# Gate products over 512 rows, spectrum sums on GpSimd, and early loads in another order

## The chip, the cores and the metric

One core of one Trainium2 chip. The metric is device time in microseconds (us) of one execution, the median of nine. "The profile" is one execution taken by the hardware profiler. Its clock starts at the first instruction of the program.

## The reference, cut to what matters

```
xn = layernorm(x)                               # x: 2048 rows x 640, bf16
A  = irfft2(rfft2(xn) * (w_r + 1j * w_i))       # over rows and columns; w: 2048 x 321
B  = ((xn @ w_gate) * (xn @ w_up)) @ w_down     # 640 -> 1536 -> 640
out = x + A + B
```

A (the filter branch) and B (the gated branch) both read xn and are independent until the last sum.

## The kernel before, in words

Each step is a *task*: a name, an engine or two, a cost in nanoseconds from a table, a priority, and the buffers that it reads and writes. A planner (class `_Sched`) runs on the host while the program is built. It lays the tasks on PE, ACT, DVE, GpSimd (POOL) and the SP queue by those costs, hands out the eight PSUM banks, and writes the waits. On the chip each engine then runs its list **in the planner's order**: an instruction whose input is late holds back all that stands behind it on that engine. Numbers behind a name are a block of 128 rows, a group, or a spectrum tile.

- **Loads.** SP issues `ld_x0` to `ld_x5` (blocks 0, 1, 2, 3, 4 to 7, 8 to 15) mixed with the weight loads `ld_gw…`, then tables (`ld_sm`, one load on ACT's queue, holds the identity and two small matrices; `ld_fd`, `ld_tf`, `ld_g`, `ld_ti`), filter rows `ld_w0…` to `ld_w3…`, and only then the transposes `xt4` to `xt15`. Later filter rows `ld_w4…` on wait for a ring of four slots.
- **Layernorm.** Blocks 0 to 7: `bn`, `ag` on DVE (L769 to L775). Blocks 8 to 15: `sm`, `sq` on ACT (L756, L762). Then `ve`, `sd`, `rs`, `sub`, `mul` (L788 to L810).
- **Transposed xn.** Blocks 0 to 3 by PE (`T0`, L828; copied out by `eT0`, L709/L710), blocks 4 to 15 by DMA (`xt`, L816).
- **Gated branch.** `GU` (L951): for one of twelve tiles of 128 gate features and a chunk of rows, five matmuls give gate and five give up, side by side in **one** PSUM bank. Chunks are 128, 128 and then seven times 256 rows. ACT copies the bank out (`eG`, L709), and for each pair of feature tiles DVE multiplies gate by up (`H`, L966). `GU` has a low priority and fills PE where the other branch waits. Last comes `ACC` (L1172): twelve matmuls of 320 columns for each block and half.
- **Filter branch, forward.** `S1` to `S5` on DVE (L865 to L899) and `R` on PE (L912; reads the second matrix of `sm`) for eight pairs of blocks.
- **Filter branch, middle, for tiles t = 0 to 15.** `D` on PE (L994), `eD` on ACT, `C` on PE (L1015 to L1018), `WM` on DVE (L1030, L1033: times the filter, reads PSUM), `CB` on DVE (L1045 to L1049: sums and differences of the four products), `NG` on ACT (L1054 to L1056: negated copies), `IA` on PE (L1070, L1071), `eIA` on ACT. The products lie in a ring of two, the results of `CB` and `NG` in a ring of two.
- **Filter branch, back.** `I` on PE (L1099), `eI` on ACT into a ring of two (`TC`), `V1` to `V5` on DVE for each pair of blocks, `IV` on PE (L1180: adds A into the bank of `ACC`), `FIN` on DVE (L1187: adds x), stores.

The early part of the step that the change moves to GpSimd is:

```
c.e.tensor_tensor(v_y[:, r2, 512:768], p01[:, 0:256], p10[:, 0:256], _OP.add)               # L1045
c.e.scalar_tensor_tensor(v_y[:, r2, 896:961], p01[:, 256:321], -1.0, ...)                   # L1046
c.e.tensor_tensor(v_y[:, r2, 768:833], p00[:, 256:321], p11[:, 256:321], _OP.subtract)      # L1048
return c.e.tensor_tensor(v_y[:, r2, 256:512], p00[:, 0:256], p11[:, 0:256], _OP.subtract)   # L1049
```

Of the kernel before, what the change touches and what calls it, by code (L numbers as in the profile page):

```python
# [15 lines left out]
_DMA_LAT = 1000.0  # L16
_DMA_ISSUE = 440.0
# [488 lines left out]
_CHUNKS = ((0, 1), (1, 1), (2, 2), (4, 2), (6, 2), (8, 2), (10, 2), (12, 2), (14, 2))  # L506
_LP = 321
_SN = math.sin(2.0 * math.pi / 5.0)
# [8 lines left out]
def _d_dve(n):  # L517
    return n * 1.04 + 65.0


def _d_dve_psum(n):
    return n * 1.04 + 70.0
# [14 lines left out]
def _d_act(n):  # L537
    return n * 0.833 + 80.0
# [8 lines left out]
def _build(nc, A_x, A_w_r, A_w_i, B_w_gate, B_w_up, B_w_down, out, opts=None):  # L547
# [3 lines left out]
    with es:  # L551
# [8 lines left out]
        sch.caps = {"glu": opts.get("cap_glu", 2), "acc": opts.get("cap_acc", 4), "fill": 1}  # L560
        lay = {}
# [43 lines left out]
        b_p = alloc("P", 2 * 4 * 2 * _LP)  # L605
        b_y = alloc("Y", 2 * 1024)
        o_end = max(o_end, cur[0])
        cur[0] = o_3
        b_tc = alloc("TC", 2 * 2560)
        b_vt = alloc("VT", 2 * 2048)  # L610
# [44 lines left out]
        v_p = V("P").bitcast(_F32).rearrange("p (r w c l) -> p r w c l", r=2, w=2, c=2)  # L655
        v_y = V("Y").rearrange("p (r n) -> p r n", r=2)
        v_tc = V("TC").bitcast(_F32).rearrange("p (r s u n) -> p r s u n", r=2, s=5, u=2)
# [54 lines left out]
        dma("ld_sm", V("SM"), d_sm.rearrange("p t n -> p (t n)"), 128 * 768, [(b_sm, None)], prio=0.002, q="act")  # L712
# [34 lines left out]
        for gi, (b0, nb) in enumerate(_X_LOADS):  # L747
            dma("ld_x%d" % gi, v_x[:, b0:b0 + nb, :], xv[:, b0:b0 + nb, :], 128 * nb * 1280,
                [(b_x, ("s", b0, b0 + nb))], prio=(0.0, 0.01, 0.02, 0.03, 0.042, 0.06)[gi])
        muls = {}  # L750
        for gi, (b0, nb) in enumerate(_LN_GROUPS):
            pbase = 1.0 + 0.05 * gi if gi < 4 else opts.get("ln_prio", 5.99) + 0.05 * (gi - opts.get("ln_lead", 3))
            for b in range(b0, b0 + nb):
# [13 lines left out]
                else:  # L767
                    def em_bn(c, b=b):
                        c.e.bn_stats(v_st[:, b, 0:6], v_x[:, b, 0:320])  # L769
                        return c.e.bn_stats(v_st[:, b, 6:12], v_x[:, b, 320:640])  # L770
                    T("bn%d" % b, "dve", 800.0, em_bn, reads=[(b_x, ("s", b, b + 1))],
                      writes=[(b_st, ("b", b, b + 1))], prio=pbase)
# [3 lines left out]
                    T("ag%d" % b, "dve", 130.0, em_ag, reads=[(b_st, ("b", b, b + 1))],  # L776
                      writes=[(b_mv, ("b", b, b + 1))], prio=pbase)
            if b0 >= opts.get("act_stats", 8):
                def em_mb(c, sl_=slice(b0, b0 + nb)):
                    c.e.tensor_copy(v_mv[:, sl_, 0], v_m32[:, sl_])  # L780
                    return c.e.tensor_scalar(v_mv[:, sl_, 1], v_ss[:, sl_], 1.0 / _D, None, _OP.mult)
                T("mb%d" % b0, "dve", 160.0, em_mb, reads=[(b_m32, ("b", b0, b0 + nb)), (b_ss, ("b", b0, b0 + nb))],
                  writes=[(b_mv, ("b", b0, b0 + nb))], prio=pbase)
# [5 lines left out]
            T("ve_%d" % gi, "dve", 80.0, em_ve, reads=[(b_mv, gk)], writes=[(b_ve, gk)], prio=pbase - 0.006)  # L789
# [3 lines left out]
            T("sd_%d" % gi, "act", 120.0, em_sd, reads=[(b_ve, gk)], writes=[(b_sd, gk)], prio=pbase - 0.006)  # L793
# [3 lines left out]
            T("rs_%d" % gi, "dve", 80.0, em_rs, reads=[(b_sd, gk)], writes=[(b_rs, gk)], prio=pbase)  # L797

            for b in range(b0, b0 + nb):
# [4 lines left out]
                T("sub%d" % b, "dve", 290.0, em_sub, reads=[(b_mv, ("b", b, b + 1))],  # L804
# [6 lines left out]
                muls[b] = T("mul%d" % b, ("dve", "act") if b >= 4 else "dve", {"dve": 290.0, "act": _d_act(640) + 93}, em_mul, reads=[(b_rs, ("b", b, b + 1))],  # L811
                  writes=[(b_x, ("s", b, b + 1))], prio=pb)

                if b >= opts.get("xt_dma", 4):
                    def em_xt(c, b=b):
                        return c.e.dma_start_transpose(v_xt[:, :, b * 128:(b + 1) * 128], v_x[:, b, :])  # L816
                    T("xt%d" % b, "sp", opts.get("xt_issue", 1500.0), em_xt, reads=[(b_x, ("s", b, b + 1))],
                      writes=[(b_xta, ("s", b * 128, (b + 1) * 128)), (b_xtb, ("s", b * 128, (b + 1) * 128))], prio=pb, nbytes=128 * 1280)
                    continue
# [11 lines left out]
                t0 = T("T0_%d" % b, "pe", 5 * _d_mm(128), em_t0, reads=[(b_x, ("s", b, b + 1)), (b_sm, None)],  # L831
                       prio=pb, bank="pair" if b < opts.get("e0_split", 2) else "single", cls="a")

                if b < opts.get("e0_split", 2):
# [9 lines left out]
                    hold(t0, es_)  # L844
                    continue
# [10 lines left out]
        for g in range(8):  # L856
# [46 lines left out]
            for u in range(2):  # L903
                def em_r(c, gr=gr, u=u):
                    bk = bank_of(c.t)
                    ins = None
                    for k, (f, o) in enumerate(((0, 1), (1, 0), (1, 1), (0, 0), (2, 0))):
# [8 lines left out]
                       reads=[(b_f, ("r", 3 * gr, 3 * gr + 3)), (b_sm, None)], prio=pf, bank="pair", cls="a")  # L916
# [18 lines left out]
        units = sorted((max(c_at[ci], w_at[ft + 1]), ci, ft) for ci in range(len(_CHUNKS)) for ft in range(0, 12, 2))  # L935
        for ui, (at_, ci, ft0) in enumerate(units):
# [6 lines left out]
            for u in range(2):  # L943
                ft = ft0 + u

# [8 lines left out]
                gu = T("GU_%d_%d" % (ft, b0), "pe", 10 * _d_mm(n), em_gu,  # L954
# [10 lines left out]
            def em_h(c, ft0=ft0, rr=rr, n=n, rows=rows):  # L965
                return c.e.tensor_tensor(v_ht[:, ft0:ft0 + 2, rows], v_gbf[:, rr, :, 0:n], v_gbf[:, rr, :, n:2 * n],  # L966
                                         _OP.mult)
            T("H_%d" % ui, "dve", _d_dve_tt16(2 * n), em_h,
# [4 lines left out]
        for q in range(2):  # L973
            dma("ld_ti%d" % q, v_ti[:, 8 * q:8 * q + 8], d_ti[:, 8 * q:8 * q + 8], 128 * 8 * 512,
                [(b_wd, ("e", 2048 * q, 2048 * q + 2048))], prio=9.0 + 0.3 * q)

        for t in range(16):
            pq = 10.0 + 0.05 * t
            ar = t % 3
            r2 = t % 2  # L980
            wr = t % _NW
            for w_ in range(2):
                for h in range(2):
# [3 lines left out]
                        semkey=("w", wr), after=[wpad])  # L987
# [34 lines left out]
            def em_wm(c, tc=tc, r2=r2, wr=wr):  # L1022
                bk = bank_of(tc)
                ins = None
                for h in range(2):
# [3 lines left out]
                    for w in range(2):  # L1029
                        c.e.tensor_tensor(  # L1030
                            v_p[:, r2, w, :, 128 * h:128 * h + 128].rearrange("p c (m k) -> p c m k", k=4),
                            xh.rearrange("p c (m k) -> p c m k", k=4), wv[:, w].unsqueeze(1).to_broadcast([128, 2, 32, 4]), _OP.mult)
                ins = c.e.tensor_tensor(  # L1033
                    v_p[:, r2, :, :, 256:321], ps[:, bk:bk + 2, 256:321].unsqueeze(1).to_broadcast([128, 2, 2, 65]),
# [4 lines left out]
                   writes=[(b_p, ("r", r2, r2 + 1))], prio=pq - 0.001, frees=tc)  # L1039
            hold(tc, wm)  # L1040

            def em_cb(c, r2=r2):
                p00, p01, p10, p11 = (v_p[:, r2, 0, 0], v_p[:, r2, 0, 1], v_p[:, r2, 1, 0], v_p[:, r2, 1, 1])

                c.e.tensor_tensor(v_y[:, r2, 512:768], p01[:, 0:256], p10[:, 0:256], _OP.add)  # L1045
                c.e.scalar_tensor_tensor(v_y[:, r2, 896:961], p01[:, 256:321], -1.0, p10[:, 256:321], _OP.mult,  # L1046
                                         _OP.subtract)
                c.e.tensor_tensor(v_y[:, r2, 768:833], p00[:, 256:321], p11[:, 256:321], _OP.subtract)  # L1048
                return c.e.tensor_tensor(v_y[:, r2, 256:512], p00[:, 0:256], p11[:, 0:256], _OP.subtract)  # L1049
            T("CB_%d" % t, "dve", 2 * _d_dve(256) + 2 * _d_dve(65), em_cb,  # L1050
              reads=[(b_p, ("r", r2, r2 + 1))], writes=[(b_y, ("r", 2 * r2, 2 * r2 + 1))], prio=pq - 0.001)

            def em_ng(c, r2=r2):
                c.e.activation(v_y[:, r2, 0:256], v_y[:, r2, 512:768], _ACTF.Copy, scale=-1.0)  # L1054
                c.e.activation(v_y[:, r2, 833:896], v_y[:, r2, 897:960], _ACTF.Copy, scale=-1.0)
                return c.e.activation(v_y[:, r2, 961:1024], v_y[:, r2, 769:832], _ACTF.Copy)  # L1056
            T("NG_%d" % t, "act", _d_act(256) + 2 * _d_act(63), em_ng,
              reads=[(b_y, ("r", 2 * r2, 2 * r2 + 1))], writes=[(b_y, ("r", 2 * r2 + 1, 2 * r2 + 2))],
              prio=pq - 0.001)

            def em_ia(c, t=t, r2=r2):
                bk = bank_of(c.t)
                ins = None
                for k in range(5):
                    if k < 4:
                        l1, l2 = v_y[:, r2, 256 + k:768:4], v_y[:, r2, k:512:4]
                    else:
                        l1, l2 = v_y[:, r2, 768:896], v_y[:, r2, 896:1024]
# [4 lines left out]
            ia = T("IA_%d" % t, "pe", 10 * _d_mm(128), em_ia, reads=[(b_y, ("r", 2 * r2, 2 * r2 + 2)), (b_wd, ("e", 256 * t, 256 * t + 256))],  # L1073
# [11 lines left out]
        for f0, f1 in _WD_LOADS:  # L1085
            dma("ld_wd%d" % f0, v_wd[:, f0:f1], wdv[:, f0:f1], 128 * (f1 - f0) * 1280,
                [(b_wd, ("e", 640 * f0, 640 * f1))], prio=18.0 if f0 < 7 else 9.6)
        for a in range(16):
# [15 lines left out]
            gr = (a // 2) % 2  # L1104
            un = a % 2

            def em_ei(c, ti=ti, gr=gr, un=un):
                bk = bank_of(ti)
                return copy_on(c, v_tc[:, gr, :, un, :],
                               psflat[:, bk * 512: bk * 512 + 640].rearrange("p (s n) -> p s n", s=5))  # L1110
            ei = T("eI_%d" % a, ("act", "dve"), {"dve": _d_dve_psum(640), "act": _d_act(640)}, em_ei,
                   writes=[(b_tc, ("r", 2 * gr + un, 2 * gr + un + 1))], prio=pa - 0.001, frees=ti)
# [5 lines left out]
            def em_v1(c, gr=gr):  # L1118
                b1r, b1i, b2r, b2i = [v_tc[:, gr, i].rearrange("p u n -> p (u n)") for i in range(4)]
# [5 lines left out]
            T("V1_%d" % b_, "dve", 4 * _d_dve(256), em_v1, reads=[(b_tc, ("r", 2 * gr, 2 * gr + 2))],  # L1125
              writes=[(b_vt, ("r", gr, gr + 1))], prio=pa - 0.001)

            def em_v2(c, gr=gr):
                a_ = v_tc[:, gr, 4].rearrange("p u (o b) -> p (u o) b", o=2)
# [3 lines left out]
              reads=[(b_vt, ("r", gr, gr + 1)), (b_tc, ("r", 2 * gr, 2 * gr + 2))],  # L1133
# [25 lines left out]
        for a in range(16):  # L1159
# [4 lines left out]
            for hf in range(2):  # L1164
# [14 lines left out]
                def em_iv(c, ag2=ag2, a=a, sl3=sl3):  # L1179
# [3 lines left out]
                       reads=[(b_v, ("a", a, a + 1)), (b_sm, None)], prio=pc + 0.01 + 0.001 * hf - 22.0, after=[ag2])  # L1183
# [13 lines left out]
        sch.affinity = opts.get("affinity", 600.0)  # L1197
# [79 lines left out]
```

## Time and profile before

| | |
|---|---|
| median of nine runs | 213.32 us (212.78 to 214.1) |
| the profiled execution | 214.05 us; span of its instructions 212.3 us |
| busy, share of the span | PE 96%, DVE 87%, ACT 57%, POOL 0% |
| granted PE clock | 1.000 |
| stage 0 to 15.18 us | first loads, layernorm of blocks 0 to 3, first `GU` |
| stage 15.18 to 88.79 us | rest of layernorm, `S`/`R`, `GU` up to the first `D` |
| stage 88.79 to 143.50 us | the sixteen tiles of the middle, `GU` between them |
| stage 143.50 to 209.67 us | `I`, the last `GU`, `V`, `ACC` |
| stage 209.67 to 212.30 us | last `FIN` and stores |

How to read it: PE's matmuls are pipelined, so a matmul's listed duration overlaps the next one's. What a run of matmuls takes is read from one start to the next, as the chain that ended last does. Idle time of an engine costs only where PE, or the end, waits for it.

### The profile page before, as it was taken

How to read it: one execution, taken by the hardware profiler on the slowest of the kernel's cores; microseconds unless marked ns; L12 is line 12 of the kernel's file. 1: busy time of each engine (PE TensorE's matmuls, PEld its weight loads, DVE VectorE, ACT ScalarE, POOL GpSimd, SP SyncE). 2: the span in 40 equal slices, each digit the busy share in tenths (PEclk: the TensorE clock that was granted, in tenths of full speed). 3: DMA queues.
4: the chain of work that ended last, by engine and by line, in shares of the span. 5: the costliest groups of instructions: out<-in, count | busy, mean ns of one | idle time of the engine just before them, and what ended most of it. 6: DMA issues, size and time to landing. Idle time of an engine off the chain costs nothing.

```text
span 212.3 us, 5204 instructions
## 1 busy us (share of the span) xinstructions
PE 202.9 (96%) x2044; PEld 169.6 (80%) x2044; DVE 185.2 (87%) x536; ACT 122.0 (57%) x281; POOL 0.2 (0%) x4
## 2 busy tenths in 40 slices
PE   8799999699999999989999999999999899999994
PEld 8789899588898998978888888898766677667773
DVE  3699989799999989389999999947999999999821
ACT  2375899699866756778999897786222202200000
POOL 0000000000000000000000000000000000000000
PEclk9999999999999999999999999999999999999999
DMA  6999999531133000002224223025033223222411
GB/s 188 302 341 396 385 302 204 110 62 31 34 61 59 8 3 0 0 11 57 60 54 119 60 62 90 3 62 154 3 106 97 64 61 110 80 76 64 127 47 46
DMA packets 30456, 21.74 MB, mean 102 GB/s; under 512 B 10336, under 2 KB 29408, under 8 KB 30304
## 3 DMA queue, kind: packets, MB, share of 16 engines
q1 hardware_dynamic: 28320, 20.34, 35.5%
q10 hardware_dynamic: 2112, 1.08, 2.0%
q8 instruction: 16, 0.26, 0.5%
q14 instruction: 8, 0.07, 0.1%
HBM read 16.82 MB, written 2.62 MB: 92 GB/s over the span
## 4 chain that ended last, share of the span: by engine, by line
PE 63%; DVE 22%; DMA 7%; issue 3%; ACT 1%; SPq 1%; DVEq 0%
PE ps L951 38%; PE ps L1172 12%; DMA arena<-in_A_x_dram 4%; DMA arena<-arena 3%; PE ps L1070 2%; PE ps L1071 2%; DVE arena L1187 2%; PE ps L994 2%; PE ps L912 2%; DVE arena L1144 1%; DVE arena L1145 1%; SPq L703 1%; DVE arena L1153 1%; DVE arena L966 1%; DVE arena L1137 1%
## 5 line engine op out<-in xcount | busy, mean ns | idle before, releaser
L709 ACT ACTIVATE arena<-ps 128x512 bf16<-128x512 f32 (+5 forms) x189 | 99.9, 572 | 55.9 <-PE ps L1099 28.2
L951 PE MATMUL ps<-arena 128*128 128x256 bf16 (+1 forms) x1080 | 112.8, 261 | 3.2 <-DMA arena<-arena 1.9
L951 PEld LDWEIGHTS ps<-arena 128*128 128x128 bf16 x1080 | 93.6, 98 | 14.5 <-DMA arena<-arena 2.1
L1172 PE MATMUL ps<-arena 128*128 128x320 bf16 x384 | 56.5, 299 | 0.3 <-DVE arena L1187 0.3
L1172 PEld LDWEIGHTS ps<-arena 128*128 128x128 bf16 x384 | 37.2, 98 | 14.7 <-DVE arena L1187 0.7
L966 DVE TENSOR_TENSOR arena<-arena 128x512 bf16<-128x512 bf16 (+1 forms) x54 | 21.1, 391 | 11.1 <-ACT arena L709 11.0
L1030 DVE TENSOR_TENSOR arena<-ps,arena 128x256 f32<-128x256 f32 x64 | 22.6, 418 | 0.0
L1187 DVE TENSOR_TENSOR arena<-ps,arena 128x320 bf16<-128x320 f32 x32 | 15.6, 486 | 6.7 <-PE ps L1180 6.7
L1070 PE MATMUL ps<-arena 128*128 128x128 bf16 x80 | 10.6, 219 | 0.0
L1071 PE MATMUL ps<-arena 128*128 128x128 bf16 x80 | 10.6, 219 | 0.0
L1180 PE MATMUL ps<-arena 128*128 128x320 bf16 x32 | 9.1, 300 | 0.6 <-DVE arena L1154 0.4
L1070 PEld LDWEIGHTS ps<-arena 128*128 128x128 bf16 x80 | 8.7, 112 | 0.5
L865 DVE TENSOR_TENSOR arena<-arena 128x384 f32<-128x384 bf16 x16 | 8.8, 553 | 0.0
L1071 PEld LDWEIGHTS ps<-arena 128*128 128x128 bf16 x80 | 8.7, 112 | 0.0
L769 DVE BATCH_NORM_STATS2 arena<-arena 128x6 f32<-128x320 bf16 x8 | 3.9, 491 | 3.7 <-DMA arena<-in_A_x_dram 3.7
L1033 DVE TENSOR_TENSOR arena<-ps,arena 128x260 f32<-128x260 f32 x16 | 7.1, 445 | 0.0
L1045 DVE TENSOR_TENSOR arena<-arena 128x256 bf16<-128x256 f32 x16 | 6.8, 423 | 0.2
L1054 ACT ACTIVATE arena<-arena 128x256 bf16<-128x256 bf16 x16 | 6.6, 414 | 0.3 <-DVE arena L1049 0.2
L1049 DVE TENSOR_TENSOR arena<-arena 128x256 bf16<-128x256 f32 x16 | 6.7, 421 | 0.0
L866 DVE TENSOR_TENSOR arena<-arena 128x256 f32<-128x256 bf16 x16 | 6.7, 420 | 0.0
L1152 DVE TENSOR_TENSOR arena<-arena 128x640 bf16<-128x640 f32 x8 | 6.6, 821 | 0.1
L762 ACT ACTIVATE arena<-arena 128x640 bf16<-128x640 bf16 x8 | 6.6, 827 | 0.0
(71 smaller groups left out, 213.1 us busy)
## 6 DMA issues: line engine op xcount, KB each, us to landing
arena<-in_A_x_dram SPq DMA_DIRECT2D x20, 160.0 KB, 2.4
out_dram<-arena SPq DMA_DIRECT2D x32, 80.0 KB, 1.6
arena<-c_tf SPq DMA_DIRECT2D x4, 384.0 KB, 11.3
arena<-in_A_w_r_dram SPq DMA_DIRECT2D x32, 40.1 KB, 2.3
arena<-in_A_w_i_dram SPq DMA_DIRECT2D x32, 40.1 KB, 2.2
arena<-in_B_w_gate_dram SPq DMA_DIRECT2D x4, 320.0 KB, 7.8
arena<-in_A_x_dram SPq DMA_DIRECT2D x1, 1280.0 KB, 12.2
arena<-c_ti SPq DMA_DIRECT2D x2, 512.0 KB, 14.0
```

The source lines that it names most:

```text
L709: return c.e.activation(dst, src, _ACTF.Copy)
L865: c.e.tensor_tensor(uo[:, o, :, 0:3, :], v_xb[:, b:b + 2, 0:6:2, :], v_xb[:, b:b + 2, 5:10:2, :], op)
L951: ins = c.e.matmul(ps[:, bk, w * n:(w + 1) * n], v_gw[:, w, j, ft, :], v_xt[:, j, rows], start=(j == 0), stop=(j == 4))
L966: return c.e.tensor_tensor(v_ht[:, ft0:ft0 + 2, rows], v_gbf[:, rr, :, 0:n], v_gbf[:, rr, :, n:2 * n], _OP.mult)
L1030: c.e.tensor_tensor(v_p[:, r2, w, :, 128 * h:128 * h + 128].rearrange("p c (m k) -> p c m k", k=4), xh.rearrange("p c (m k) -> p c m k", k ...
L1033: ins = c.e.tensor_tensor(v_p[:, r2, :, :, 256:321], ps[:, bk:bk + 2, 256:321].unsqueeze(1).to_broadcast([128, 2, 2, 65]), v_w[:, wr, :, 0 ...
L1045: c.e.tensor_tensor(v_y[:, r2, 512:768], p01[:, 0:256], p10[:, 0:256], _OP.add)
L1070: c.e.matmul(dst, l1, v_ti[:, t, 0, :], start=True, stop=False)
L1071: ins = c.e.matmul(dst, l2, v_ti[:, t, 1, :], start=False, stop=True)
L1172: ins = c.e.matmul(ps[:, bk, 0:320], v_ht[:, ft, a * 128:(a + 1) * 128], v_wd[:, ft, sl3], start=(ft == 7), stop=False)
L1180: return c.e.matmul(ps[:, bank_of(ag2), 0:320], v_sm[:, 2, :], v_v[:, a, sl3], start=False, stop=True)
L1187: return c.e.tensor_tensor(v_out[:, a % 2, sl3], ps[:, bk, 0:320], v_xr[:, xs, sl3], _OP.add)
```

## The change

Four parts; in each, the planner's cost table and limits change with it, so that the whole order is planned anew.

1. **Chunks.** Rows 512 to 2047 are taken in three chunks of 512. For these, one `GU` is five matmuls of 512 columns that fill a whole bank with gate *or* up (named `GU_f_row_0` and `_1`); `H` covers one feature tile and 512 rows. A chunk needs four transposed blocks before its first matmul.
2. **Sums on GpSimd.** `CB` keeps the two operations of 256 columns (L1045, L1049) and goes to POOL. The two of 65 columns become `CD` on DVE. `NG` waits for both. The rings of products and of results become three deep, and so does `TC`.
3. **Early loads.** `ld_x1` goes ahead of the first weights. `ld_sm` is split: the identity stays on ACT's queue, the rest (`ld_sm1`) goes on SP behind `ld_x5`. `ld_ti`, all `ld_w` and `ld_wd` wait for the last layernorm `mul15`, so the transposes stand ahead of them on SP. `bn` is two tasks, and the second of block 1 waits for the copy of the first transposed block.
4. **Planner.** Entries of its cost table are changed (most of those of DVE, ACT and DMA are raised); at most two tasks of class "a" hold banks at once; ACT is preferred over DVE for copies by 1500 ns, not 600.

In the order that results, PE runs `T0_1` behind `GU_3_0`, `R_0` behind `GU_3_2`, and `I_6`, `I_7` ahead of `ACC_0_0`. ACT runs `sm8` between the two copies of `GU_2_2` and `GU_3_2`. POOL runs `CB_0` to `CB_15`.

```diff
-_CHUNKS = ((0, 1), (1, 1), (2, 2), (4, 2), (6, 2), (8, 2), (10, 2), (12, 2), (14, 2))
+_CHUNKS = ((0,1),(1,1),(2,2),(4,4),(8,4),(12,4))
...
+        sch.caps["a"] = opts.get("cap_a", 2)
...
-        b_p = alloc("P", 2 * 4 * 2 * _LP)
-        b_y = alloc("Y", 2 * 1024)
+        b_p = alloc("P", 3 * 4 * 2 * _LP)
+        b_y = alloc("Y", 2 * _YS)
+        b_y3 = alloc("Y3", _YS, at=lay["STAT"][0])
...
+        b_tc3 = alloc("TC3", 2560, at=lay["GBF"][0])
...
-        dma("ld_sm", V("SM"), d_sm.rearrange("p t n -> p (t n)"), 128 * 768, [(b_sm, None)], prio=0.002, q="act")
+        dma("ld_sm0", v_sm[:, 0, :], d_sm[:, 0, :], 128 * 256, [(b_sm, ("t", 0, 1))], prio=0.002, q="act")
+        dma("ld_sm1", v_sm[:, 1:3, :], d_sm[:, 1:3, :], 128 * 512, [(b_sm, ("t", 1, 3))], prio=0.25)
...
+                if nb == 4:
+                    def em_gu4(c, ft=ft0, w=u, rows=rows):
+                        bk = bank_of(c.t)
+                        for j in range(5):
+                            ins = c.e.matmul(ps[:, bk, :], v_gw[:, w, j, ft, :], v_xt[:, j, rows], start=(j == 0),
+                                             stop=(j == 4))
+                        return ins
...
+                c.e.tensor_tensor(v_y[ar][:, 512:768], p01[:, 0:256], p10[:, 0:256], _OP.add)
+                return c.e.tensor_tensor(v_y[ar][:, 256:512], p00[:, 0:256], p11[:, 0:256], _OP.subtract)
+            ce = opts.get("cb_eng", "pool")
+            T("CB_%d" % t, ce, {"dve": 2 * _d_dve(256), "pool": opts.get("cb_pool", 1600.0)}, em_cb,
...
-                        semkey=("w", wr), after=[wpad])
+                        semkey=("w", wr), after=[wpad, muls[opts.get("w_after", 15)]])
...
-        sch.affinity = opts.get("affinity", 600.0)
+        sch.affinity = opts.get("affinity", 1500.0)
```

## The prediction

> **What bounds the kernel now.** I read the page first: PE is busy throughout, DVE nearly so.
>
> ```profile
> PE 202.9 (96%) x2044; PEld 169.6 (80%) x2044; DVE 185.2 (87%) x536; ACT 122.0 (57%) x281; POOL 0.2 (0%) x4
> PE   8799999699999999989999999999999899999994
> DVE  3699989799999989389999999947999999999821
> ```
>
> Busy is no proof of being the limit, so I took the lengths of PE's runs from the chain that ended last (start, length, what).
>
> ```profile
> 22.15 0.56 PE ps L912 x10
> 98.84 1.09 PE ps L951 x10
> 191.90 1.63 PE ps L1172 x12
> ```
>
> Ten matmuls of 128 columns take 0.56 us, ten of 256 take 1.09, twelve of 320 take 1.63: 0.056, 0.109 and 0.136 each, that is 0.417 ns a column and 2.5 ns a matmul. In the same view `C` (four of 321) takes 0.55 and `IV` 0.137. Now the work from 15.18 us, where the last `T0` has ended, stage by stage, against the windows.
>
> ```profile
> 15.18:88.79 73.61, 71.53 (x753) 63.35 (x751) 67.40 (x201) 57.32 (x123) 0.00 (x0) 1.00 0.48 123
> 88.79:143.50 54.71, 54.13 (x596) 47.74 (x594) 49.20 (x161) 46.49 (x123) 0.00 (x0) 1.00 0.23 56
> 143.50:209.67 66.17, 64.32 (x518) 46.50 (x516) 58.35 (x139) 11.37 (x18) 0.00 (x0) 1.00 0.27 82
> ```
>
> First stage: 14 `GU` of 128 rows (7.8), 53 of 256 (57.9), 16 `R` (4.5): 70.2 of 73.6 us. Middle: 16 x (`D` 0.28 + `C` 0.55 + `IA` 0.56) = 22.2 and 29 `GU` (31.7): 53.9 of 54.7. Last: 16 `I` (4.5), two `GU` (2.2), 32 `ACC` with `IV` (56.7): 63.4 of 66.2. So PE has work for 187.5 of 194.5 us, and **all that can be won behind the start is 7.0 us of stalls (3.4, 0.8, 2.8) and the fixed part of the matmuls**. Where the stalls lie, PE's and SP's timelines say:
>
> ```profile
> 9.54 4.43 PE L951 MATMUL ps<-arena 128*128 128x128 bf16 x70 [0.18 <-DMA arena<-in_B_w_gate_dram]
> 21.98 0.72 PE L912 MATMUL ps<-arena 128*128 128x128 bf16 x10
> 39.75 6.91 PE L951 MATMUL ps<-arena 128*128 128x256 bf16 x60 [1.85 <-DMA arena<-arena]
> 158.82 0.45 PE L1180 MATMUL ps<-arena 128*128 128x320 bf16 x2 [0.42 <-DVE arena L1154]
> 161.32 0.72 PE L1099 MATMUL ps<-arena 128*128 128x128 bf16 x10 [0.29 <-DVE arena L1131]
> 29.21 1.18 SPq L703 DMA_DIRECT2D arena<-in_A_w_r_dram  x2
> 32.25 21.58 SPq L816 DMA_TRANSPOSE arena<-arena  x8
> ```
>
> PE stands 2 us at 38 to 39.75 for the first transpose, which SP issued at 32.25 behind the filter loads; later it waits for `V5` and `V2` on DVE.
>
> **Chunks of 512.** A matmul of 512 columns is 0.417 x 512 + 2.5 = 216 ns, so a `GU` of five takes 1.08 where ten of 256 took 1.092: 72 of them save 0.9 us. Bank copies and `H` stay at 512 columns. But the first one needs blocks 4 to 7, not 4 and 5. DVE's queue says when the last, `mul7`, comes: from `S1_0` (14.7, as before) the list up to it is `S_0` 5.5, `S1` to `S3` of group 1 4.2, eight `bn` at 0.40, eight `H` at 0.21 and three at 0.33, `ag`, four `sub` and `mul` at 0.30, small ones: 19 us, so 34 to 35.5 with some waits for ACT. With 2.6 us to land (the median of the page) `xt7` is there at 37 to 38, and PE arrives at 37.5 to 39 (below). The 2.0 us stall goes; its cover is thin.
>
> **Early loads.** Two answers in opposite directions. `GU_0_0` starts about 0.9 earlier (7.8 to 6.9), because the copy it waits for no longer stands behind `bn` of block 1. But `T0_1` now stands behind `GU_2_0`, whose weights land at 9.5 (the row at 9.54): PE idles from 8.0 to 9.4, then 0.5 more for the copies of `T0_1`. Summed row by row, the last `T0` ends at 15.4 instead of 15.18: **+0.2**. Then `R_0` needs `ld_sm1`, queued behind the 1280 KB of x:
>
> ```profile
> arena<-in_A_x_dram SPq DMA_DIRECT2D x1, 1280.0 KB, 12.2
> arena<-c_fd SPq DMA_DIRECT2D x1, 160.5 KB, 11.1
> ```
>
> Issued at 12.06 and 13.54, these landed at 24.3 and 24.6; `ld_sm1` comes between them. PE reaches `R_0` at 15.4 + 6 x 0.56 + 4 x 1.09 = 23.1: **+1.2**, a stall that was not there (`R` started at 21.98). `sm8` waits for the same x on ACT from 22.6 on, with a bank copy behind it, and PE's next `GU` wait for that: +0.6 more. Moving the filter loads behind the transposes costs nothing: 19 loads at 0.6 us on SP after the last transpose (67 us) are issued by 80, and `C_0` comes at about 88; if the transposes slipped 6 us it would begin to cost. `R_2` to `R_6` meet DVE within half a microsecond either way: +0.6, from 0 to 2.
>
> First stage after: 7.8 + 12 x 1.092 + 41 x 1.08 + 4.5 = 69.7, stalls 2.4 (3.4 before).
>
> **Sums on GpSimd.** DVE loses two rows of 0.34 us each tile:
>
> ```profile
> L1045 DVE TENSOR_TENSOR arena<-arena 128x256 bf16<-128x256 f32 x16 | 6.8, 423 | 0.2
> L1049 DVE TENSOR_TENSOR arena<-arena 128x256 bf16<-128x256 f32 x16 | 6.7, 421 | 0.0
> L1054 ACT ACTIVATE arena<-arena 128x256 bf16<-128x256 bf16 x16 | 6.6, 414 | 0.3 <-DVE arena L1049 0.2
> ```
>
> 16 x 0.67 = 10.7 us leave DVE, at a place where PE is the limit (0.8 us of stalls), so this buys no time there by itself. What POOL takes no row shows; its only rows set one column. Bounds: 0.67 for both if it kept DVE's pace; 1.66 if it read one operand at a time at ACT's 0.41 for 256. I take 1.6, near the upper row, and carry 3.3 as the rival's. The path that counts is from `C_t` to `IA_t`: `WM` 1.75, `CB` 1.6, `NG` 0.6, handovers 0.4, queueing on DVE and ACT 0.8: 5.2 us. In PE's order at the densest place (t = 7 to 11) there stand between them `D` 3, `GU` 3, `IA` 2, `C` 2 = 6.3 us, so 1.1 us of cover; a lower `CB` gains nothing. But the pace there is one tile in 2.47 us (1.39 + one `GU`), where ACT's timeline gives `eD` 0.71 + `eIA` 0.62 + `NG` 0.60 + a bank copy 0.55 = 2.48 and SP's 4 x 0.62 for filter rows: no room. Middle stage after: 22.2 + 27 x 1.08 = 51.4, stalls 1.5 (0.5 to 4).
>
> The Trainium skill, GPSIMD Engine Reference, section 3.1, gives about 2.6 cycles an element for a two-input operation; an estimate from it is 1.2 us for the pair, and the sum stays as it is. Against this change speaks SBUF — State Buffer, section "Who interferes with whom": a VectorE operation with two SBUF inputs and a GpSimd operation that reads SBUF shut each other out for a whole instruction. `CD` and `H` are such; one GpSimd operation of 0.6 us waited for in each tile would put 9.6 us back on DVE, 49 us of the stage's 51.4, and still not make it the end. No row here shows it.
>
> **Rings of three.** Last stage: `I_6`, `I_7` go early and `I` waits for a `V2` two pairs back. DVE needs 5.5 for `V` and 1.2 to 1.6 for `FIN` a pair, PE 7.6. Laying both lists out from `I_0` I find waits of 0.1 and 0.2 at `IV`, 0.5 and 0.4 at `I`: 1.2 us instead of 2.8. Work: 4.5 + 4 x 1.08 + 56.7 = 65.5.
>
> **Sum.** 15.4 + 69.7 + 51.4 + 65.5 = 202.0, stalls 2.4 + 1.5 + 1.2 = 5.1, tail 2.6 as before: a span of 209.7 against 212.3. The profiled execution took 214.05, 1.75 more than its span, so 211.45; it lies 0.7 above the median, so the median should be **210.7**.
>
> **Rivals.** (1) *The stalls all but go* (1.5 us in all: `ld_sm1` lands early, DVE keeps ahead of `R`): 207.1. For it: every stage has spare DVE time on average; against it: the landing of x. (2) *Slower by GpSimd*: at 3.3 us a `CB`, 16 x 3.3 = 53 us is the middle stage's 52.9, and the path becomes 6.9, 0.6 over its cover. From there POOL is the bound: at 3.6 the stage is 57.6 plus about 1 to fill, 5.7 over forecast, 216.4. For it: no row of POOL exists and DVE's two-input rows run at the same time; against: 3.3 is five times DVE's rows. (3) *One wait for another*: `mul7` late by 2 us, `R` late on DVE, the start at +0.2: the first stage keeps 4.5 us of stalls, 2.1 more than forecast: 212.8. (4) *The change doesn't do what it says* can't be where POOL's list holds all `CB`.
>
> **How the numbers follow.** 0.3% (0.64 us) is about what a measurement of this kernel can tell from no change. Chances: forecast 0.52, rival 1 0.16, rival 2 and its like 0.23, rival 3 0.09. Faster 0.68, same 0.09, slower 0.23. The range for 8 in 10 goes from rival 1, 207.1, into rival 2, 215.5.
>
> **What would show it.** Right: `R_0` (L912 by its new number) starting at 24.3 to 24.7 with PE idle before it; no idle over 0.5 before the first matmul of 512 columns, at 37.5 to 39.5; ten matmuls of 512 in 2.16 us; the first `I` at 139 to 141.5; POOL start to start 0.6 to 0.9 within a pair. Wrong: POOL busy over 50 us with PE waiting for ACT's `NG`; `xt7` landing after 40.

## The result and the profile after

The change made the kernel slightly **slower**: 213.96 us (213.66 to 214.51, fifteen runs) against 213.0 for the kernel before (47 runs, the nine above among them); ratio 1.0044, 95% interval 1.0034 to 1.0055. Forecast: 210.7, faster.

The page of the profile after, the lines that answer to those of before:

```profile
PE 202.2 (95%) x1684; PEld 135.2 (64%) x1684; DVE 185.5 (87%) x504; ACT 122.1 (58%) x281; POOL 22.5 (11%) x36
PE   8889999999999999999997889999999999999994
DVE  4699899999999997399899997966999999999921
```

Two 256-column sums a tile have left DVE, and DVE is busy for 185.5 us, where it was 185.2. And PE has a hole in the middle that it did not have. The windows, by the same three stages (from the end of the last `T0`, here 15.58, to `D_0`, to `I_0`, to PE's end; length, then PE, PEld, DVE, ACT, POOL busy):

```profile
15.58:86.27 70.69, 70.36 (x548) 43.58 (x546) 66.73 (x200) 56.80 (x122) 0.00 (x0) 1.00 0.47 126
86.27:143.10 56.83, 53.02 (x440) 32.40 (x439) 50.01 (x128) 45.92 (x121) 22.32 (x32) 1.00 0.22 54
143.10:209.27 66.17, 65.78 (x517) 46.83 (x516) 57.92 (x138) 12.73 (x21) 0.00 (x0) 1.00 0.27 82
```

Stalls, as the sum of the time by which each start-to-start step of PE's matmuls exceeds the matmul's own length (0.417 ns a column + 2.5 ns), to about 0.1: 3.5, 1.0 and 2.9 us before, 1.2, **5.6** and 0.9 after. The first and last stage won about 4.3 us, the middle gave 4.6 back. What PE waited for there, by its timeline (the last field is the idle time and its releaser; L1066 is `WM`'s last row):

```profile
117.36 1.25 PE L962 MATMUL ps<-arena 128*128 128x512 bf16 x5 [1.57 <-DVE arena L1066]
123.17 0.73 PE L1027 MATMUL ps<-arena 128*128 128x128 bf16 x10 [0.93 <-DVE arena L1066]
```

These two are 2.5 of the 5.6 us; the view of PE's waits names 0.6 more for `WM` and 0.7 for `NG` on ACT. So PE waits mostly for DVE's `WM`, in the stage from which DVE's work was taken. The groups of the middle stage say why; first `CD`'s two rows before (L1046, L1048), in a second fence after (L1086, L1088), with `H` (L998), `WM` (L1063) and the sums on POOL:

```profile
L1048 DVE TENSOR_TENSOR arena<-arena 128x65 bf16<-128x65 f32 x16 | 3.6, 224 | 0.0
L1046 DVE SCALAR_TENSOR_TENSOR arena<-arena 128x65 bf16<-128x65 f32 x16 | 3.6, 223 | 0.0
```

```profile
L1063 DVE TENSOR_TENSOR arena<-ps,arena 128x256 f32<-128x256 f32 x64 | 22.5, 411 | 0.0
L1079 POOL TENSOR_TENSOR arena<-arena 128x256 bf16<-128x256 f32 x16 | 11.6, 725 | 0.0
L1078 POOL TENSOR_TENSOR arena<-arena 128x256 bf16<-128x256 f32 x16 | 11.3, 707 | 117.7 <-DVE arena L1066 117.7
L1088 DVE TENSOR_TENSOR arena<-arena 128x65 bf16<-128x65 f32 x16 | 11.3, 705 | 0.0
L998 DVE TENSOR_TENSOR arena<-arena 128x512 bf16<-128x512 bf16 x14 | 7.5, 535 | 7.9 <-ACT arena L714 7.9
L1086 DVE SCALAR_TENSOR_TENSOR arena<-arena 128x65 bf16<-128x65 f32 x16 | 6.3, 393 | 0.3
```

The same 65 columns took 224 ns and take 705, as long as the row of 256 columns on POOL beside them. DVE's and POOL's timelines of one tile show it:

```profile
93.80 0.66 DVE L1086 SCALAR_TENSOR_TENSOR arena<-arena 128x65 bf16<-128x65 f32 x1
94.38 0.77 DVE L1088 TENSOR_TENSOR arena<-arena 128x65 bf16<-128x65 f32 x1
95.07 1.07 DVE L1063 TENSOR_TENSOR arena<-ps,arena 128x256 f32<-128x256 f32 x3
```

```profile
93.62 0.75 POOL L1078 TENSOR_TENSOR arena<-arena 128x256 bf16<-128x256 f32 x1 [1.16 <-DVE arena L1066]
94.34 0.73 POOL L1079 TENSOR_TENSOR arena<-arena 128x256 bf16<-128x256 f32 x1
```

In this tile each row of `CD` ends 0.09 us behind the POOL row that was running, and the next row of `WM` starts 0.01 us behind POOL's second. So it goes in six tiles; in the ten others `CD`'s first row starts 0.05 us ahead of POOL and takes its 0.23, and only the second is held up. From `CD`'s first start to its last end it is 0.81 us in the ten tiles and 1.35 in the six, 1.01 on average. All of `CB` (the two long sums included) took 1.03 before. **GpSimd relieved DVE of 16 x 0.02 us.** And three rows of `H` that met POOL took 0.96 us each where `H` took 0.42 before, 1.6 us in all: DVE has more busy time in the stage than before, 50.0 us where it was 49.2. `WM`, which reads one operand from PSUM, is untouched: the 21 of its rows (L1063) that overlap a POOL row last 406 to 413 ns, the others 407 to 425. This agrees with the rule of the Trainium skill, SBUF — State Buffer, section "Who interferes with whom", which the prediction weighed.

### The profile page after: what moved, and what is told of

Same layout as the page of the kernel before. It is cut to its first block, busy times and chain, and to the rows that moved or that the text cites. A ratio compares the mean times of both kernels' runs of the same rounds, so it can differ in the third digit from the quotient of the medians.

```text
span 212.0 us, 4504 instructions
## 1 busy us (share of the span) xinstructions
PE 202.2 (95%) x1684; PEld 135.2 (64%) x1684; DVE 185.5 (87%) x504; ACT 122.1 (58%) x281; POOL 22.5 (11%) x36
## 4 chain that ended last, share of the span: by engine, by line
PE 61%; DVE 21%; SPq 6%; DMA 5%; ACT 3%; POOL 1%; issue 1%; ACTq 0%; DVEq 0%
PE ps L962 26%; PE ps L1213 22%; DVE arena L1063 9%; PE ps L982 6%; SPq L708 6%; DMA arena<-c_sm 5%; DVE arena L1088 3%; ACT arena L714 3%; DVE arena L1066 2%; PE ps L924 2%; PE ps L1138 2%; PE ps L1221 2%; DVE arena L1086 2%; DVE arena L998 2%; POOL arena L1079 1%
## 5 line engine op out<-in xcount | busy, mean ns | idle before, releaser
L962 PE MATMUL ps<-arena 128*128 128x512 bf16 x360 | 83.1, 379 | 1.6 <-DVE arena L1066 1.6
L962 PEld LDWEIGHTS ps<-arena 128*128 128x128 bf16 x360 | 33.6, 98 | 37.9 <-DVE arena L1066 1.9
L1213 PEld LDWEIGHTS ps<-arena 128*128 128x128 bf16 x384 | 37.3, 98 | 14.4
L982 PE MATMUL ps<-arena 128*128 128x128 bf16 (+1 forms) x360 | 28.2, 237 | 1.5 <-DMA arena<-in_B_w_gate_dram 1.0
L982 PEld LDWEIGHTS ps<-arena 128*128 128x128 bf16 x360 | 24.9, 98 | 4.0 <-DMA arena<-in_B_w_gate_dram 1.3
L998 DVE TENSOR_TENSOR arena<-arena 128x512 bf16<-128x512 bf16 x36 | 16.7, 464 | 10.6 <-ACT arena L714 10.6
L1078 POOL TENSOR_TENSOR arena<-arena 128x256 bf16<-128x256 f32 x16 | 11.3, 707 | 117.7 <-DVE arena L1066 117.7
L1063 DVE TENSOR_TENSOR arena<-ps,arena 128x256 f32<-128x256 f32 x64 | 22.5, 411 | 0.0
L1109 PE MATMUL ps<-arena 128*128 128x128 bf16 x80 | 10.7, 220 | 1.3 <-ACT arena L1095 0.7
L1109 PEld LDWEIGHTS ps<-arena 128*128 128x128 bf16 x80 | 8.6, 111 | 5.2 <-ACT arena L1095 2.3
L1079 POOL TENSOR_TENSOR arena<-arena 128x256 bf16<-128x256 f32 x16 | 11.6, 725 | 0.0
L1088 DVE TENSOR_TENSOR arena<-arena 128x65 bf16<-128x65 f32 x16 | 11.3, 705 | 0.0
L1110 PE MATMUL ps<-arena 128*128 128x128 bf16 x80 | 10.7, 219 | 0.0
L777 DVE BATCH_NORM_STATS2 arena<-arena 128x6 f32<-128x320 bf16 x16 | 7.2, 478 | 3.4 <-DMA arena<-in_A_x_dram 3.1
L1110 PEld LDWEIGHTS ps<-arena 128*128 128x128 bf16 x80 | 8.8, 112 | 0.7
L1027 PE MATMUL ps<-arena 128*128 128x128 bf16 (+1 forms) x80 | 6.8, 219 | 0.9 <-DVE arena L1066 0.9
```

The lines of the kernel that those rows point to most:

```text
L962: ins = c.e.matmul(ps[:, bk, :], v_gw[:, w, j, ft, :], v_xt[:, j, rows], start=(j == 0), stop=(j == 4))
L982: ins = c.e.matmul(ps[:, bk, w * n:(w + 1) * n], v_gw[:, w, j, ft, :], v_xt[:, j, rows], start=(j == 0), stop=(j == 4))
L998: return c.e.tensor_tensor(v_ht[:, ft0, rows], v_gbf[:, rr, 0, :], v_gbf[:, rr, 1, :], _OP.mult)
L1063: c.e.tensor_tensor(v_p[:, ar, w, :, 128 * h:128 * h + 128].rearrange("p c (m k) -> p c m k", k=4), xh.rearrange("p c (m k) -> p c m k", k ...
L1079: return c.e.tensor_tensor(v_y[ar][:, 256:512], p00[:, 0:256], p11[:, 0:256], _OP.subtract)
L1088: return c.e.tensor_tensor(v_y[ar][:, 768:833], p00[:, 256:321], p11[:, 256:321], _OP.subtract)
```

## Experiments

Theory A: GpSimd's reads hold up `CD` (and some `H`); DVE gets no time back, and PE, in an order laid out for a relieved DVE, waits for `WM`. Rival B: the way from `C` to `IA` over GpSimd is too long. Rival C: the order is bad by itself. "Same order" means that every engine's list is kept as planned, and the edit is made behind `sch.plan`.

**1. CD first.** One wait more:

```diff
+            cb, cd = by["CB_%d" % i], by["CD_%d" % i]
+            cb.deps.add(cd)
...
```

> The changed kernel, every engine's order kept, but CB on GpSimd waits until CD of its tile has ended on DVE. Theory A: CD no longer meets its tile's CB, its two rows fall from 393 and 705 ns to about 225 each, DVE gets 0.65 us a tile back, some H may still be held up, and the middle stage's stalls fall from 5.6 to between 1 and 2.5 us: 209.3 to 211 us. Rival B: CB starts about 0.45 us later, so the way from C to IA is longer still: 214.5 or more. Rival C: 213.5 to 214.5.

Measured: **208.88 us**, ratio to the kernel before 0.9805 (0.9783 to 0.9828), 5.1 us less than the changed kernel. Its groups, and its windows for the middle stage:

```profile
L1086 DVE SCALAR_TENSOR_TENSOR arena<-arena 128x65 bf16<-128x65 f32 x16 | 3.6, 227 | 0.3
L1088 DVE TENSOR_TENSOR arena<-arena 128x65 bf16<-128x65 f32 x16 | 3.6, 222 | 0.0
```

```profile
87.31:138.97 51.66, 51.66 (x440) 32.96 (x439) 38.76 (x128) 45.30 (x121) 21.65 (x32) 1.00 0.27 59
```

`CD` is back at 0.36 us from start to end, DVE at 38.8 us where it was 50.0, PE without a hole. The gain is larger than A's range (209.3 to 211) allowed: 0.5 us of stalls are left in the stage, not 1 to 2.5. B and C fall: `CB` started later, in the same order, and the time fell. This version beats both kernels.

**2. The sums back on DVE**, same order:

```diff
+            sch.order["pool"].remove(cb)
+            dve.insert(dve.index(wm) + 1, cb)
...
```

> The changed kernel with its order on PE, ACT and SP kept as it is, and only CB put back on DVE, directly behind WM. Theory A (given back): GpSimd's reads hold up CD on DVE, so DVE never got the freed time, and PE's order, laid out for a DVE with 0.67 us less a tile, runs into WM. CB and CD then cost DVE 0.67 + 0.28 = 0.95 us a tile where the held-up CD costs 0.39 + 0.71 = 1.10, so most of the middle stage's 5.6 us of stalls stay: 212.3 to 213.7 us. Rival B (long path): the pair on GpSimd makes the way from C to IA too long; that way gets about 0.5 to 0.8 us shorter, and the stalls go: 209.3 to 211. Rival C (the order itself is bad, wherever the sums run): 213.5 to 214.5.

Measured: 213.25 us (ratio 1.0005, 0.9993 to 1.0017), middle stalls 4.9 us. As A says: a DVE that does the sums itself is as late as one that is held up by them.

**3. The sums on DVE, planned anew**, that is the other parts of the change without GpSimd:

```diff
-            ce = opts.get("cb_eng", "pool")
+            ce = opts.get("cb_eng", "dve")
```

> The changed kernel with CB on DVE, and the planner laying out the order with DVE's true load: the change without its GpSimd part. A, B and C agree here that the middle stage falls back to about the 1.0 us of stalls of the kernel before, while the 2.4 us won in the first stage, the 2.0 in the last and the 0.9 of fixed matmul parts stay: 209.2 to 210.5 us. At 212.5 or more the other parts would be worth nothing, and the prediction would be wrong in more than one step.

Measured: 213.91 us (1.0040, 1.0024 to 1.0055). All three theories missed. PE had no gate products left at the end of the stage and stood idle, and the granted clock (the last but two of the numbers) was lower behind that; the windows at that place:

```profile
140.00:145.00 5.00, 2.41 (x26) 1.53 (x23) 2.57 (x9) 3.44 (x9) 0.00 (x0) 1.00 0.24 66
145.00:149.50 4.50, 4.46 (x36) 3.62 (x37) 2.59 (x8) 3.09 (x5) 0.00 (x0) 0.62 0.61 182
```

The lower clock is not what cost most of it: in two of the nine runs it was 1.000 over the whole execution, not 0.992, and they took 213.47 and 213.88 us, the other seven 213.76 to 214.65.

**4. The same with four gate products kept for that place**, ahead of `sch.plan`:

```diff
+        for u in range(2):
+            by["GU_10_12_%d" % u].deps.add(by["C_15"])
+            by["GU_11_12_%d" % u].deps.add(by["IA_%d" % (14 + u)])
...
```

> The run with the sums on DVE and a new plan (213.91 us) showed PE idle for 1.74 and 0.89 us at the end of the middle stage, behind its last gate product, with the granted clock at 0.5 from about 145.5 to 149 us. Here the same kernel is planned with its last four gate products kept for that place (two not before C_15, two not before IA_14 and IA_15). Theory: that drain and the lower clock behind it cost 4.4 us together, and the order holds what the other parts won: 209.2 to 210.7 us. Rival: DVE's load with the sums costs PE the time all through the stage, so it comes back elsewhere: 212.5 or more.

Measured: 213.78 us (1.0035, 1.0018 to 1.0051). The clock stayed at 1.0, but 3.2 us of stalls in the middle and 3.0 in the last stage remained. The rival holds: with the sums on DVE the stage is 58.7 us long for 55.5 of PE's work (four products more than in the changed kernel lie in it), and 53.1 of it pass from the first `WM` to DVE's last sum. In these two plans the other parts of the change win nothing without a relieved DVE.

**5. A dose of DVE time** on top of experiment 1, one or two useless memsets behind each `CD`:

```diff
+                t = _Task(..., lambda c: c.e.memset(V("JK")[:, 0:640], 0.0), 0.0)
...
+                dve.insert(dve.index(cd) + 1 + k, t)
```

> CD ahead of CB as in the run at 208.88 us, every order kept, and one useless memset of 320 columns of four bytes put on DVE behind each CD (no SBUF input, some 0.25 to 0.35 us). Theory (the chain on DVE sets the middle stage): from D_0 to WM_0 3.0 us, DVE's work from WM_0 to the last CD (37.8 us there), about 2.3 us of DVE idle that stays, and 2.6 from the last CD to I_0. That reaches PE's 51.7 us only when DVE has 43.8 us, 6 more: one memset a tile gives 4 to 5.6 and is nearly free: 208.8 to 209.6 us. Rival (PE waits for each WM in turn, so every 0.3 us on DVE counts in full): 16 x 0.3 more, 212.5 to 214.

> The same with two memsets behind each CD, the second waiting for the first (0.5 to 0.75 us a tile, DVE's load about that with the sums on it, while these run unhindered on GpSimd). Theory: DVE has 46.5 to 49.5 us between WM_0 and the last CD, the stage is that plus 7.9 us, 54.4 to 57.4 instead of 51.7: 211.5 to 214.5 us, PE waiting for WM again though nothing is held up. Rival (the loss in the changed kernel is the mutual exclusion as such, not DVE's load): 208.8 to 209.8.

Measured: 211.47 us (0.9921, 0.9903 to 0.9939) and 216.67 (1.0171, 1.0147 to 1.0194). One memset took 0.325 us. PE's longest wait in the middle stage of the run with two (what waited, for what, us in total, times, longest):

```profile
PE ps L962 <- DVE arena L1066: 2.5, 3, 1.5
```

16 x 0.325 = 5.2 us of memsets cost 2.6, the next 5.2 cost all 5.2. The first lies between the two expectations, the second over A's: some of DVE's time is free, but less than the 6 us that A allowed. So DVE time that no POOL row made brings PE's waits for `WM` back: 4.6 us of them before `GU`, `IA` and `D`. DVE's lateness costs PE time however it comes about. It was not the dose's only way: 1.8 us more are waits of PE for `NG` on ACT, and ACT's `NG` waited 5.8 us for POOL's sums.

**6. GpSimd alone**, in the order of the kernel before: the two sums moved to POOL (first run), then also the wait of experiment 1 (second), then also rings of three for products and results (third):

```diff
+            sch.order["dve"].remove(cb)
+            sch.order["pool"].append(cb)
...
+            cb.deps.add(cd)
...
-            r2 = t % 2
+            r2, q2 = t % 3, t % 2
```

> The kernel before, with PE's, ACT's and SP's order kept, and only the two 256-column sums moved to GpSimd; CD stays on DVE. 13.5 us of rows leave DVE. Theory A: CD's second row grows from 224 to about 670 to 700 ns, the first on average to about 390, so DVE's time a tile goes from 0.95 only to 1.10, and an order that allowed for 0.95 on DVE stays about as it was: 212.7 to 214.2 us, no gain from the relief. Rival B: the way from C to IA is 0.5 to 0.8 us longer in an order with rings of two: 215 to 218. If GpSimd truly relieved DVE and PE's stalls hung on DVE, 212 or less.

> The kernel before, the orders of PE, ACT and SP kept, the two 256-column sums on GpSimd, and CB waiting for CD: the GpSimd part alone, without the hold-up of CD. Theory: in that order PE has only 1.0 us of stalls in the middle stage and enough gate products between the tiles, so the relief of DVE alone has little to win: 212.0 to 213.2 us. Rival (DVE alone sets the time): 211 or less. If H is still held up as in the run at 215.63: 213.5 to 214.5.

> The run at 218.12 us (order of the kernel before, sums on GpSimd, CD ahead of CB) with the products and the results in rings of three instead of two, all five orders kept. C of a tile takes over the waits of its WM, and with a ring of two WM waits for CB two tiles back. Theory (the way over GpSimd closes the ring of two): C waits for CB three tiles back, which is long done; the middle stage's 5.6 us of stalls fall to 1 or 2: 213.0 to 214.5 us. Rival (DVE's H ahead of CD, and with it CB and NG, is what is late): 216.5 to 218.

Measured: 215.63 us (1.0124, 1.0101 to 1.0146), 218.12 (1.0232, 1.0207 to 1.0257) and 217.61 (1.0212, 1.0185 to 1.0238). The first lies in B's range, over A's. It shows the hold-up again, on `H` (L966) too, which took 424 ns before:

```profile
L966 DVE TENSOR_TENSOR arena<-arena 128x512 bf16<-128x512 bf16 x15 | 10.0, 669 | 5.8 <-ACT arena L709 5.6
L1054 DVE TENSOR_TENSOR arena<-arena 128x65 bf16<-128x65 f32 x16 | 9.1, 567 | 0.0
```

The second is slower than each of its three expectations, the third is the rival's. DVE is relieved there (39 us busy of a 59 us stage in the second), and yet PE waits; two lines of the waits in the middle stage of the second, then two of the third:

```profile
PE ps L1015 <- POOL arena L1046: 2.3, 4, 0.6
DVE arena L966 <- ACT arena L709: 19.7, 15, 2.3
```

```profile
ACT arena L1059 <- POOL arena L1046: 6.9, 10, 1.2
PE ps L1075 <- ACT arena L1061: 3.1, 5, 0.9
```

In that order the way over GpSimd holds PE up, as rival B has it: `NG` on ACT (L1059) waits for POOL, PE's `IA` (L1075) for `NG`. The copies (L709) stand behind `NG` on ACT, and DVE's `H` waits 19.7 us for them where it waited 5.1 before. That the `CD` and `CB` behind such an `H` are then late in turn follows from the order of the lists; no run takes it apart. The deeper ring took away `C`'s wait for POOL but only 0.5 us of the time. So the same extra wait wins 5.1 us in one order and loses 2.5 in another.

**7. Is 208.88 one lucky order?** Experiment 1 with the planner told of the wait:

```diff
+            cd = T("CD_%d" % t, "dve", 2 * _d_dve(65), em_cd,
...
+              reads=[(b_p, ("r", ar, ar + 1))], writes=[(by, ("r", y0, y0 + 1))], prio=pq - 0.001, after=[cd])
```

> The changed kernel with CB waiting for CD, and the planner told of it, so that the order in the middle stage is laid out anew (other numbers as they are). Theory: DVE has as little work as in the run at 208.88 us, and the order knows the wait: 208.3 to 209.8 us. Rival (208.88 hangs on one lucky order): 211 or more.

Measured: 209.08 us (0.9814, 0.9791 to 0.9836). It isn't.

**8. The other parts, each undone on top of experiment 1**: `ld_sm1` ahead of the last load of x; `TC` a ring of two; the old chunks; `ld_sm`, `ld_x1` and `bn` as before:

```diff
+        sp.insert(sp.index(x5), s1)
...
-            gt = (a // 2) % 3
+            gt = (a // 2) % 2
...
-_CHUNKS = ((0,1),(1,1),(2,2),(4,4),(8,4),(12,4))
+_CHUNKS = ((0,1),(1,1),(2,2),(4,2),(6,2),(8,2),(10,2),(12,2),(14,2))
...
-        dma("ld_sm0", ...)
-        dma("ld_sm1", ...)
+        dma("ld_sm", V("SM"), d_sm.rearrange("p t n -> p (t n)"), 128 * 768, [(b_sm, None)], prio=0.002, q="act")
...
-                        bns[0].deps.add(muls[0])
-                        bns[1].deps.add(e0_first)
```

> CD ahead of CB as in the run at 208.88 us, every engine's order kept, but SP issues ld_sm1 (64 KB) ahead of the last, 1280 KB load of x instead of behind it. R_0 waited there for c_sm, 0.9 us in that profile. Theory (the prediction's price of ld_sm1): the wait goes and 0.3 to 0.9 us come out at the end: 208.0 to 208.6 us. Rival: x lands later by 64 KB, or DVE's S5 is late next, and nothing is won: 208.7 to 209.2.

> CD ahead of CB, but the ring of TC has two places again, as in the kernel before; by the plan PE's order is the same up to I_3. Theory (the prediction's price of the third place): the last stage's stalls go from 0.9 back to between 2.2 and 2.9 us: 210.1 to 211.0 us. Rival: with DVE relieved the third place is worth nothing: 208.7 to 209.2.

> CD ahead of CB, but the gate products over chunks of 256 rows as in the kernel before, planned anew. Theory (the prediction's price of the chunks): 72 times 12.5 ns, 0.9 us, more of work on PE, and up to 2 us of stall at the first transposed block, which chunks of 512 skip: 209.8 to 211.8 us. Rival: PE is not the end, or the chunks' gain is given back by waits: 208.5 to 209.2.

> CD ahead of CB, but the early part as in the kernel before: one ld_sm ahead of all on ACT's queue, ld_x1 behind the first gate weights, and no wait of block 1's bn rows for block 0. The planner's order differs in the first stage only by a few exchanged gate products. Theory (the prediction's price of the early loads: +0.2 us at the start, +1.2 at R_0, +0.6 behind it, so the reordering loses): 207.0 to 208.4 us. Rival (the reordering wins the early start of the products that the first stage's stalls, 1.2 us instead of 3.5, seem to show): 209.5 to 210.8.

Measured: 208.98 us (0.9810, 0.9794 to 0.9827), 209.42 (0.9830, 0.9812 to 0.9848), 209.91 (0.9858, 0.9835 to 0.9881) and 209.10 (0.9811, 0.9790 to 0.9832). Against 208.88: +0.1, +0.5, +1.0, +0.2; only the 1.0 of the chunks is clear of the intervals. The early reordering is worth nothing that can be measured, either way. In the run with `ld_sm1` early the rival came true, in the one with the loads as before theory and rival both missed; the ring of two lies between its two expectations, the chunks in the theory's. `R_0`'s wait, taken away, is followed by another of 0.62 us a few products later, at 27.24, on ACT's copies (`ld_sm1` early). The new cost table and limits (part 4) were not undone by themselves.

With chunks of 256 rows the 2 us of idle at the first transposed block do not come back; PE's timeline there has no idle field:

```profile
37.72 4.53 PE L982 MATMUL ps<-arena 128*128 128x256 bf16 x40
```

## Why the prediction was wrong, by its own steps

**Right.** PE's work: 69.7, 51.4 and 65.5 us forecast, 69.5, 51.2 and 65.3 measured (stage less stalls). Ten matmuls of 512 in 2.16 us. The pair on GpSimd: 1.6 taken, 1.40 measured from the first start to the last end (0.67 start to start). The estimate from the Trainium skill, GPSIMD Engine Reference, section 3.1, was 1.2; its 2.6 cycles an element and its clock of 1.2 GHz make 1.1 of 512 elements, and the measurement is above both. The way from `C` to `IA` has cover in this order: experiment 1 lengthened it and won. Chunks: 0.9 forecast, 1.0 in experiment 8. `R_0` and the first product of 512 columns, from PE's timeline after:

```profile
23.98 0.73 PE L924 MATMUL ps<-arena 128*128 128x128 bf16 x10 [0.33 <-DMA arena<-c_sm]
38.56 5.56 PE L962 MATMUL ps<-arena 128*128 128x512 bf16 x25
```

The product came in its interval and with no idle before it; `R_0` was 0.3 earlier than its interval, its wait 0.3 instead of 1.2. The first `I` came at 143.1, behind its interval of 139 to 141.5.

**The step that failed** is the last argument of "Sums on GpSimd". The sum put the hold-up of `CD` and `H` at nothing, because 9.6 us back on DVE would make 49 us of the stage's 51.4 "and still not make it the end". The size was near: the hold-up put back 10.4 us on `CD` (1.01 where it is 0.36 without POOL in its way, in sixteen tiles) and 1.6 on `H`, and DVE was busy for 50.0 us of the stage; the prediction's own numbers, 49.2 - 10.7 + 9.6, make 48.1. The windows from the first `WM` to DVE's last sum, of before, after and experiment 1, have DVE's busy time behind PE's and PEld's (47.35, 49.01, 37.78):

```profile
91.89:140.22 48.33, 47.75 (x528) 42.09 (x527) 47.35 (x157) 41.37 (x111) 0.00 (x0) 1.00 0.24 58
```

```profile
89.26:140.54 51.28, 47.48 (x395) 28.99 (x394) 49.01 (x126) 40.78 (x109) 22.32 (x32) 1.00 0.22 53
```

```profile
90.29:134.51 44.22, 44.22 (x379) 28.38 (x378) 37.78 (x126) 38.61 (x107) 20.32 (x30) 1.00 0.28 61
```

The comparison was wrong. DVE cannot use the whole stage: `WM_0` comes 3.0 us after `D_0`, and from DVE's last sum to `I_0` there are 2.6 more (`NG`, `IA`, `eIA`). Of 51.4 us that leaves 46, less than 49. 2.99 + 49.01 + 2.27 of idle + 2.56 = 56.83, the measured stage, against 51.2 of PE's work. The view of before held it already: DVE was busy for 47.35 of 48.33 us between those two points. So the sentence ahead of it, that PE is the limit at that place and a relief of DVE "buys no time there by itself", was half the truth: DVE was as full as PE, and what the other parts won could only be kept if DVE got shorter too. In experiments 3 and 4, without that, it was not kept.

**Mis-sized.** The ring's third place: 1.6 us forecast, 0.5 alone (experiment 8), which is not clear of noise, though the stage's stalls came out near the forecast (1.2; 0.9). `R_0` and `sm8`: 1.8 us of stalls that were mostly not there in this execution, so the first stage was 1.4 better than forecast. This changes from one execution to the next: in experiment 1's profile, with the same early loads, `R_0` waited 0.92 us and started at 25.01. The start: +0.2 forecast, +0.4 here, and in the profiles of the other runs that keep these loads the last `T0` ends at 15.7 to 16.1. The 2 us at the first transpose did go, but not by the chunks: with the old ones (experiment 8) they stayed away. SP issued the first transpose at 27.48 where it was 32.25, with no filter load before it, and at 27.73 with the old chunks and 26.03 with the old first loads. This points to the filter loads that were moved behind the transposes; that was not tried alone.

**The sum.** Against the forecast: start +0.2, first stage -1.4, middle +3.9, last -0.5, tail +0.1: +2.3 us of span. The other 0.9 is that the profiled execution lay 0.7 over its median before and 0.2 under it after.

**Rivals.** Rival 2 had the sign and the engine, not the mechanism: POOL was busy for 22 us, far from the 53 at which it would have been the bound. What decided was what POOL's reads do to DVE. That 213.96 lies within the range of 207.1 to 215.5 is luck: the range reached that far for rival 2, at a price of POOL that was not the one measured.

What stays open is how much a microsecond on DVE costs PE in the range between (2.6 of the first 5.2, all of the second).

## What to carry to other kernels

Before you move work from DVE to GpSimd, look at what DVE does in those moments: here DVE's operations with two operands from SBUF waited out a whole GpSimd row (65 columns took 705 ns, not 224), those that read PSUM did not, and one wait that ran the short DVE rows first was worth 5.1 us in one order and lost 2.5 in another. Compare an engine's busy time not with the stage but with the part of it between its first possible start and the last moment it is needed. An engine that is full beside the bound keeps what other edits win; look for it in the windows before you call its relief worthless.

## What was not expected of the hardware

POOL's rows pay too: in the first run of experiment 6 its second sum, about 0.72 us in most tiles, took 0.91 in four, where an `H` had got in ahead of it. And in experiment 3 two idle times of PE, 1.74 and 0.89 us within 3.4, were followed by a granted clock of 0.62 on average over the next 4.5 us, although one idle of 1.57 us in the changed kernel, and a pair of 0.56 and 1.28 within 3.7 us in experiment 4, left it at 1.0.
